# Attention with a two-layer network beside it on one core: filling matmuls at their whole length, unread products in half cycles that have none, rows of maxima sent one half cycle sooner, batches dealt by unit

## The chip, the cores and the metric

The kernel runs on one core of one Trainium2 chip. The metric is device time in microseconds (us) of one execution, lower is better. Before the change three runs took 1750.22, 1755.51 and 1757.24 us; their median is 1755.51 us. The engines are named as in the profile: PE is TensorE with its matmuls (PEld its weight loads), DVE is VectorE, ACT is ScalarE, POOL is GpSimd, and SP is SyncE, whose queue starts nearly all transfers.

## What is computed

One block of a transformer over 2048 rows of 512 numbers, in float32: a layer norm modulated by a condition, attention with 32 heads of 16 columns that share one key head and one value head, a gated residual, a second modulated layer norm, a gelu network of width 1376, and a second gated residual.

```python
mod = (_silu(c) @ w_mod).reshape(c.shape[0], 6, 1, -1)
sa, ca, ga, sb, cb, gb = (mod[:, 0], ..., mod[:, 5])
h = _layernorm(x, axis=-1) * (1 + ca) + sa
x = x + ga * _A_ref(h, A_wq, A_wk, A_wv, A_wo)     # softmax(q k^T / 4) v @ wo, 32 heads, one k and one v
h = _layernorm(x, axis=-1) * (1 + cb) + sb
x = x + gb * _B_ref(h, B_w1, B_b1, B_w2, B_b2)     # gelu(h @ w1 + b1) @ w2 + b2
```

## The kernel before the change

**Units and cycles.** After a prologue (keys, values, the first queries) the kernel runs 64 units: 8 blocks of 256 rows, and in each block 8 groups of four heads. A unit takes the 16 tiles of 128 keys in three cycles, by `GROUPS`: (3, 3), (2, 3) and (3, 2) tiles. A cycle has two half cycles. In each, PE makes score products `e` (L644, one for each key tile and each pair of heads s = 0 or 1), which ACT turns into exponentials `p` (L647), and products `m` (L542) for the maxima of a unit further on, which DVE reduces to one column (L547). An `e` or `m` product uses only 64 of the 128 rows of the array: s = 0 the upper half, s = 1 the lower. After each half cycle `pv` (L662) adds exponentials times values into the accumulator `acc`: 16 or 24 instructions in the trace. An x16 or x24 burst of `acc` on PE therefore marks the end of each half cycle.

**Filling.** While one half of the array makes the s = 1 products, the other half can do something else, and the next half cycle the other way round. What is put there is called the filling: the late query projections, and for a finished block the output projection `wo`, the second norm's transposes, and the two layers `w1` and `w2` (tiles `fill`, line L193). `compose(room)` (L1239) takes up to `room` products (256 columns each) from a queue of jobs; the room is given by `UNITS` for the three cycles of a unit. `halves` (L1491) issues the batch once on rows 0 to 63 and once on rows 64 to 127. The first filling of a half cycle waits for the exponential of the product `follow` (L1482) that closed the filling of the half before ("witness"), and for readers of the bank. Where a sum ends in a batch, `finish` (L1274) lets its reader run (ACT or DVE), after the second half's fillings; if the other sum of the bank is still under way, ACT also writes zeros there (L1285). Reductions of the last two maxima of such a half cycle are held until then.

**Order on PE.** `issue` (L1432) merges two lists by their nominal lengths: each `e` or `m` counts 1, a filling counts `AHEAD` times 0.5. With `AHEAD` = 0.75 the list of fillings runs through faster than the other one. `k` products `e` stand on the side of the filling, the rest beside it (`beside`, L1478); `k` is chosen so that the two sides have like lengths. The exponential of the last product beside the filling goes on ACT's queue only after the one of `follow`.

**A cycle with no filling** (`plain`, L1503) deals `m` and `e` of both halves in turn, and lends the filling's bank to one `m`.

**Maxima.** The maxima of a unit run ahead of its scores by 24 of 32 products (`LEAD`). When those of unit u are half done, `load_q(u + 1)` (L503) issues the eight transfers of the queries of the next unit on SP (L513 and L515, tile `qst`). When they are done, `put_max` (L566) reduces and transposes on DVE, gathers on POOL (L590, then the splits at L131 and L138) `MAX_WAIT[0]` ticks later (a tick is explained below), and sends four small transfers on SP (L585, `mh` and `ml`) `MAX_WAIT[1]` ticks after the transposition. The scores of unit u subtract these rows, so its first `e` waits for the last of them.

**Finished blocks.** When a block's last unit is done, `rest` fetches sums and outputs (`rsum` and `os`), inverts (`drs`), fetches the factors (`os<-drs`, L797), multiplies and splits on POOL (`norm`), and then feeds the filling. SP works strictly in the order of its queue: a transfer that waits for an engine, or for another transfer, holds all behind it. `later(n, fn)` calls fn after n ticks of a clock with four ticks for each cycle (two for each half cycle, one before and one after the `acc` burst).

Of the kernel before, what the change touches and what calls it, by code (L numbers as in the profile page):

```python
# [14 lines left out]
P = 128  # L15
# [14 lines left out]
MAX_WAIT = (1, 4)  # L30
QBUFS = 4
PREP = 4
BUSY = 3
BATCH = 6
GROUPS = ((3, 3), (2, 3), (3, 2))
UNITS = (16, 16, 14)
SPILL = 2
TAIL = (4, 8)
GROUP = 4
NORM_WAIT = 6  # L40
WARM = (4, 16, 2, 5)
MOD_WAIT = 3
AHEAD = 0.75
STIR = ((0, 4, 8, 12), (16, 32, 48, 0))


# [5 lines left out]
def adaln_mqa_mlp(  # L52
# [57 lines left out]
    ks = const.tile([P, S], F32R, name="ks")  # L110
# [35 lines left out]
    def later(n, fn):  # L146
        if draining[0]:
            fn()
        else:
            pending.append((clock[0] + n, fn))  # L150
# [38 lines left out]
    def half(one, s, behind=()):  # L189
# [4 lines left out]
        for other in behind:  # L194
# [3 lines left out]
    fill = {"bank": None, "next": 0, "flight": [None, None], "unread": [False, False], "bits": [True, True], "zero": [False, False],  # L198
            "reads": [], "last": None}
# [300 lines left out]
    NU = len(units)  # L500
# [123 lines left out]
    waiting = []  # L624
# [129 lines left out]
    def rest(b, fast):  # L754

        rp = wts_pool["rest"]
        row0, w = blocks[b]
        spread = ["m", "e", "m", "e", "m", "e", "v"] if fast else ["x"]
        turn = [0]

        def bank():
            turn[0] += 1
            tag = spread[turn[0] % len(spread)]
            return ebank() if tag == "e" else dict(tag=tag, bufs=3 if tag == "m" else 1)

        oss, ons = {}, {}

        def fetch():

            n = H * w // P  # L770
            rsum = att.tile([P, n], F32, name=f"rsum{b}", tag="rsum", bufs=1)
            nc.sync.dma_start(out=rsum, in_=do[b][:, :, 16, :].rearrange("q c (t n) -> (q c) t n", n=n))
            fetch_heads(0)

            def invert():
                nc.vector.reciprocal(out=rsum, in_=rsum)
                later(1, scatter)

            def scatter():
                nc.sync.dma_start(out=drs[b].rearrange("h (t n) -> (h t) n", n=n), in_=rsum)  # L780
                fetch_factors(0)

            later(4, invert)

        def fetch_heads(hf):

            os_ = oss[hf] = att.tile([P, 2, KD, HQ], F32, name=f"os{b}_{hf}", tag="opk", bufs=1)
            cols = slice(hf * HQ, (hf + 1) * HQ)
            for g in range(KD):
                src = do[b][2 * g:2 * g + 2, :, 0:16, cols].rearrange("q c r n -> (q c) r n")  # L790
                nc.sync.dma_start(out=os_[:, 0, g, :], in_=src)

        def fetch_factors(hf):
            cols = slice(hf * HQ, (hf + 1) * HQ)
            for g in range(KD):
                src = drs[b][8 * g:8 * g + 8, cols].unsqueeze(1).to_broadcast([8, 16, HQ])
                nc.sync.dma_start(out=oss[hf][:, 1, g, :], in_=src)  # L797
            later(7, lambda: norm(hf))

        def norm(hf):  # L800
            if fast:
                g = KD - 1
                split(state["on"][0][:, g, :], state["on"][1][:, g, :], state["os"][:, 0, g, :], nc.scalar, nc.vector)
                return
            onH = att.tile([P, KD, HQ], F32R, name=f"onH{b}_{hf}", tag="xH", bufs=2)
            onL = att.tile([P, KD, HQ], F32R, name=f"onL{b}_{hf}", tag="xL", bufs=2)
            ons[hf] = (onH, onL)
            os_ = oss.pop(hf)
            for g in range(KD):
                nc.gpsimd.tensor_tensor(out=os_[:, 0, g, :], in0=os_[:, 0, g, :], in1=os_[:, 1, g, :], op=ALU.mult)  # L810
            split(onH, onL, os_[:, 0], nc.gpsimd, nc.gpsimd)
            if (hf + 1) * HQ < w:
                later(6, lambda: (fetch_heads(hf + 1), fetch_factors(hf + 1)))
            ready[hf] = clock[0] + NORM_WAIT

        ready = {}
        later(*((4, lambda: norm(0)) if fast else (2, fetch)))
        return rest_steps(b, fast, rp, bank, ons, ready)

# [384 lines left out]
    pulled = []  # L1204
# [34 lines left out]
    def compose(cap):  # L1239

        batch, ends, used = [], [], 0
        while True:
            if not pulled:
                op = pull()
                if op is None:
                    break
                pulled.append(op)
            one, n = pulled[0]
            left = sum(units_of(b_) for _, _, b_ in one.ops[n:])
            if n == 0:  # L1250
                where = (0, 1) if one.wide else (fill["next"],)
                if any(fill["unread"][r] for r in where) or used and used + SPILL >= cap:
                    break
                begin = not any(fill["flight"])
                if begin:
                    fill["bits"][:] = [False, False]
                assert not one.wide or begin
                for r in where:
                    assert not fill["bits"][r] or fill["zero"][r]
                    fill["flight"][r], fill["unread"][r], fill["bits"][r], fill["zero"][r] = one, True, True, False  # L1260
                one.where = where[0]
                fill["next"] = 0 if one.wide else 1 - where[0]
            if used + units_of(one.ops[n][2]) > cap + (SPILL if used + left <= cap + SPILL else 0):
                break
            sub_, a, b_ = one.ops[n]
            ps = one.place()
            batch.append((ps if sub_ is None else ps[:, sub_], a, b_, n == 0 and begin, n == len(one.ops) - 1))
            used += units_of(b_)
            if n == len(one.ops) - 1:
                ends.append(one)  # L1270
            pulled.clear()
        return batch, ends, used / 2

    def finish(ends, ins):  # L1274
# [14 lines left out]
    first = [sum(size[:u]) for u in range(NU + 1)]  # L1289
    mp = Max()  # L1290
# [170 lines left out]
    behind = None  # L1461
    for u in range(NU):
        kt = 0
        for (nx, ny), room in zip(GROUPS, UNITS):
            X, Y = list(range(kt, kt + nx)), list(range(kt + nx, kt + nx + ny))
            kt += nx + ny
            goal = lead[u] + (lead[u + 1] - lead[u]) * kt / NKT
# [7 lines left out]
            def exps(s, which):  # L1475
                return [(1.0, lambda kt_=kt_: sexp(u, kt_, s)) for kt_ in which]

            def beside(s, which):  # L1478

                return exps(s, which[:-1]) + [(1.0, lambda: sexp(u, which[-1], s, None if followed else waiting))]  # L1480

            def follow(s, kt_):  # L1482

# [5 lines left out]
            ended, followed = [], []  # L1489
# [22 lines left out]
            batch, ends, long = compose(room) if behind else ([], [], 0)  # L1512
            if batch:
                k = min(max(1, round((n / 2 + nx + ny - long) / 2)), nx + ny - 1)
                which = X + Y
# [99 lines left out]
```

## Time and profile before

| | |
|---|---|
| runs | 1750.22, 1755.51, 1757.24 us (median 1755.51) |
| the profiled execution | 1755.45 us, its span 1753.6 us |
| mean granted PE clock | 0.969 |
| busy | PE 94%, PEld 64%, DVE 79%, ACT 73%, POOL 39% |
| cycles of the loop | 192, of which 16 without filling (15 after the first) |

The span is the time from the first to the last instruction. A "window" is a stretch of the span with the busy time of each engine in it and the granted clock; windows were laid on the ends of `acc` bursts, so that their lengths are the lengths of cycles or half cycles.

### The profile page before, as it was taken

To read this page: it belongs to the slowest core of one execution; us is meant where nothing else is said; L and a number is where in the kernel's file an instruction comes from. 1 tells how busy PE (TensorE), PEld (TensorE's weight loads), DVE (VectorE), ACT (ScalarE), POOL (GpSimd) and SP (SyncE) were. 2 spreads that over 40 slices of the span, in tenths; PEclk is the share of its full clock that TensorE was granted. 3 is DMA by queue.
4 is the path that set the end of the run, shared out by engine and by line. 5 is a ranking of instruction groups with operands and counts; after the bars stand their busy time and mean duration, and the time that the engine had idled before them with its cause. 6 is when DMAs were issued, how large, how long until landed. Compare 5 with 4: busy or idle time off the path is not lost.

```text
span 1753.6 us, 44436 instructions
## 1 busy us (share of the span) xinstructions
PE 1641.2 (94%) x17936; PEld 1125.2 (64%) x17936; DVE 1380.2 (79%) x2419; ACT 1271.5 (73%) x2564; POOL 682.5 (39%) x1194
## 2 busy tenths in 40 slices
PE   7999997999989998989989999889989999888998
PEld 4477763567765676657766677657766677555767
DVE  7888887888878887988878888788878788776524
ACT  6488876778766886778766887678867787666843
POOL 6335344556213462046322462135512362123630
PEclk9999999999998999999998999999999999988999
DMA  8125322212120211213012111203012121211241
GB/s 266 43 97 176 120 87 72 84 48 79 32 74 24 75 56 41 71 28 102 14 44 71 60 63 47 73 13 98 30 49 69 41 84 31 64 36 57 74 145 43
DMA packets 83138, 121.81 MB, mean 69 GB/s; under 512 B 19615, under 2 KB 56223, under 8 KB 82677
## 3 DMA queue, kind: packets, MB, share of 16 engines
q1 hardware_dynamic: 82916, 118.97, 20.8%
q8 instruction: 141, 2.31, 0.5%
q14 instruction: 65, 0.52, 0.1%
q10 hardware_dynamic: 16, 0.00, 0.0%
HBM read 91.13 MB, written 27.27 MB: 68 GB/s over the span
## 4 chain that ended last, share of the span: by engine, by line
PE 84%; ACT 5%; DVE 5%; SPq 2%; DMA 2%; issue 1%; POOL 1%; DVEq 0%; POOLq 0%
PE acc L662 27%; PE m L542 20%; PE fill L193 18%; PE e L644 15%; DVE mx L547 4%; ACT p L647 3%; SPq L585 1%; DMA qst<-ml 1%; PE w2ps L182 1%; PE w1ps L182 1%; DMA xt<-in_A_x_dram 1%; SPq L513 1%; PE fill L182 1%; PE kps L163 1%; ACT tt L1005 0%
## 5 line engine op out<-in xcount | busy, mean ns | idle before, releaser
L547 DVE TENSOR_REDUCE mx<-m 128x1 f32<-128x512 f32 x2016 | 1259.0, 684 | 278.9 <-PE m L542 156.9
L647 ACT ACTIVATE p<-e 128x512 f32<-128x512 f32 x2048 | 1087.6, 600 | 358.6 <-PE e L644 323.8
L644 PE MATMUL e<-qst,ks 64*128 64x512 f32 x2048 | 782.1, 442 | 67.1 <-DMA qst<-ml 41.2
L542 PE MATMUL m<-ks,qst 64*128 64x512 f32 x2016 | 809.6, 431 | 26.3 <-DVE mx L547 25.8
L662 PE MATMUL acc<-p,va 128*32 128x256 f32 x8192 | 534.6, 391 | 0.0
L542 PEld LDWEIGHTS m<-ks,qst 64*128 64x128 f32 x2016 | 369.6, 189 | 207.2 <-DVE mx L547 149.1
L644 PEld LDWEIGHTS e<-qst,ks 64*128 64x128 f32 x2048 | 340.6, 189 | 146.0 <-ACT p L647 86.6
L662 PEld LDWEIGHTS acc<-p,va 128*32 128x32 f32 x8192 | 230.0, 111 | 231.1 <-issue 110.9
L590 POOL TENSOR_SCALAR mt<-turned 8x32 f32<-8x32 f32 x256 | 53.1, 208 | 584.6 <-DVE turned L596 572.6
L193 PE MATMUL fill<-h2H,w1t 64*128 64x256 f32 x1232 | 233.6, 284 | 0.0
L193 PEld LDWEIGHTS fill<-h2H,w1t 64*128 64x128 f32 x1232 | 190.0, 186 | 0.1
L193 PE MATMUL fill<-h2L,w1t 64*128 64x256 f32 x616 | 173.1, 281 | 0.0
L193 PE MATMUL fill<-w2H,gH 64*128 64x256 f32 x560 | 164.0, 293 | 0.0
L193 PE MATMUL fill<-w2H,gL 64*128 64x256 f32 x560 | 162.4, 290 | 0.0
L193 PE MATMUL fill<-w2L,gH 64*128 64x256 f32 x558 | 158.4, 284 | 0.0
L193 PEld LDWEIGHTS fill<-h2L,w1t 64*128 64x128 f32 x616 | 114.7, 186 | 0.2 <-ACT p L647 0.2
L193 PEld LDWEIGHTS fill<-w2H,gL 64*128 64x128 f32 x560 | 107.4, 192 | 0.4
L193 PEld LDWEIGHTS fill<-w2H,gH 64*128 64x128 f32 x560 | 107.5, 192 | 0.0
L193 PEld LDWEIGHTS fill<-w2L,gH 64*128 64x128 f32 x558 | 106.8, 191 | 0.0
L1011 POOL TENSOR_TENSOR tt<-tt,z 128x256 f32<-128x256 f32 x77 | 56.5, 734 | 73.1 <-ACT tt L1005 73.1
L193 PE MATMUL fill<-woL,onH 64*128 64x256 f32 x224 | 63.7, 284 | 0.0
L193 PE MATMUL fill<-woH,onL 64*128 64x256 f32 x224 | 63.5, 283 | 0.0
(201 smaller groups left out, 1780.9 us busy)
## 6 DMA issues: line engine op xcount, KB each, us to landing
w1t<-dw SPq DMA_DIRECT2D x82, 512.0 KB
qst<-dq SPq DMA_DIRECT2D x384, 32.0 KB
do<-oc SPq DMA_DIRECT2D x64, 128.0 KB
dw<-w1s SPq DMA_DIRECT2D x11, 512.0 KB
xt<-in_A_x_dram SPq DMA_DIRECT2D x4, 1024.0 KB
dq<-qH SPq DMA_DIRECT2D x16, 256.0 KB
dq<-qL SPq DMA_DIRECT2D x16, 256.0 KB
x<-in_A_x_dram SPq DMA_DIRECT2D x8, 512.0 KB
```

The lines of the kernel that those rows point to most:

```text
L163: nc.tensor.matmul(ps, a, b_, start=begin and n == 0, stop=end and n == last)
L182: ins = nc.tensor.matmul(ps, a, b_, start=first_, stop=last_, **how)
L193: ins = nc.tensor.matmul(ps, a[rows], b_[rows], start=first_ and s == 0, stop=last_ and s == 1, skip_group_check=True)
L513: nc.sync.dma_start(out=raw(qst[64 * s + r:64 * s + r + 16]), in_=dq[h][g][part, a0 + s][:, :, cols])
L542: nc.tensor.matmul(m, qsts[u][rows, j, t * P:(t + 1) * P], ks[rows, kc * 512:(kc + 1) * 512], start=True, stop=True)
L547: nc.vector.tensor_reduce(out=self.mx[u][:, i, kc:kc + 1], in_=m, axis=AX.X, op=ALU.max)
L585: ring.dma_start(out=raw(dst), in_=raw(src[2 * T * s:2 * T * (s + 1), :].unsqueeze(1)))
L590: nc.gpsimd.tensor_scalar(out=mt[:, g:g + 32], in0=turned[g:g + 4 * T, :], scalar1=1.0, scalar2=0.0, op0=ALU.mult, op1=ALU.add)
L644: nc.tensor.matmul(e, ks[rows, kt * P:(kt + 1) * P], qst[rows].rearrange("p j n -> p (j n)"), start=True, stop=True)
L647: ins = nc.scalar.activation(slot(i), e, AF.Exp, scale=0.25)
L662: ins = nc.tensor.matmul(accs[u][32 * cidx:32 * cidx + 32, :], va[:, kt, :], slot(slots[u, kt, s])[:, j * w:(j + 1) * w], start=kt == 0, s ...
L1011: nc.gpsimd.tensor_tensor(out=tt, in0=tt, in1=z, op=ALU.mult)
```

## The change

- `AHEAD` goes from 0.75 to 1.0: a filling counts with its whole length when the order on PE is merged.
- In `compose`, a batch that would be empty, with no sum under way and maxima still to come, gets ten products of the keys with themselves that nobody reads (`IDLE`). They go through `halves` like any filling. With this 191 of the 192 cycles have a batch; seven of those hold only such products (in units 9, 11, 18, 27, 35, 51 and 59).
- `MAX_WAIT[1]` goes from 4 to 2: the four transfers `mh`, `ml` are put on SP's queue two ticks, one half cycle, sooner.
- The waits of a finished block shrink: `invert` from 4 to 3, `norm` from 7 to 5, `NORM_WAIT` from 6 to 5.
- `UNITS` depends on the unit: 12, 12, 12 products up to unit 8; 16, 16, 16 from 9; 16, 14, 14 from 22; 16, 16, 16 from 45.
- In `beside`, the last exponential is no longer put behind `follow`'s where k is over 1.

```diff
-MAX_WAIT = (1, 4)
+MAX_WAIT = (1, 2)
...
-UNITS = (16, 16, 14)
+UNITS = ((0, (12, 12, 12)), (9, (16, 16, 16)), (22, (16, 14, 14)), (45, (16, 16, 16)))
 SPILL = 2
+IDLE = 10
...
-NORM_WAIT = 6
+NORM_WAIT = 5
...
-AHEAD = 0.75
+AHEAD = 1.0
...
-            later(4, invert)
+            later(3, invert)
...
-            later(7, lambda: norm(hf))
+            later(5, lambda: norm(hf))
...
                 op = pull()
                 if op is None:
+                    if not batch and not any(fill["flight"]) and mp.done < first[NU]:
+                        idle = Sum([(None, ks[:, 0:P], ks[:, 0:256])] * IDLE, lambda one: None)
+                        pulled.extend((idle, i) for i in range(IDLE))
+                        continue
                     break
...
-            pulled.clear()
+            pulled.pop(0)
...
-        for (nx, ny), room in zip(GROUPS, UNITS):
+        for (nx, ny), room in zip(GROUPS, [rooms for since, rooms in UNITS if since <= u][-1]):
...
-                return exps(s, which[:-1]) + [(1.0, lambda: sexp(u, which[-1], s, None if followed else waiting))]
+                return exps(s, which[:-1]) + [(1.0, lambda: sexp(u, which[-1], s, None if followed or k > 1 else waiting))]
```

On SP's queue the change moves the rows of maxima past other transfers where a block has just been finished. What stands between the rows of unit 16 and those of unit 18 in program order:

```text
before: rows(16) | do rsum os(x4) out drs os<-drs(x4) loads(19) | rows(17) | do loads(20) | rows(18)
after:  rows(16) | loads(18) do rsum os(x4) out | rows(17) | drs os<-drs(x4) loads(19) do | rows(18)
```

## The prediction

> **What bounds the kernel now.** First the page: the span, busy time, and the chain that ended last by line.
>
> ```profile
> span 1753.6 us, 44436 instructions
> ...
> PE 1641.2 (94%) x17936; PEld 1125.2 (64%) x17936; DVE 1380.2 (79%) x2419; ACT 1271.5 (73%) x2564; POOL 682.5 (39%) x1194
> ...
> PE acc L662 27%; PE m L542 20%; PE fill L193 18%; PE e L644 15%; DVE mx L547 4%; ACT p L647 3%; SPq L585 1%; DMA qst<-ml 1%; PE w2ps L182 1%; PE w1ps L182 1%; DMA xt<-in_A_x_dram 1%; SPq L513 1%; PE fill L182 1%; PE kps L163 1%; ACT tt L1005 0%
> ```
>
> PE's products of the unit loop are the chain; the other engines appear with a few per cent each. As busy time says little about PE, I then laid windows on cycles (their ends are the ends of `acc` bursts): (2, 3) and (3, 2) of unit 29 and (3, 3) of unit 30, all with 16 fillings; (3, 2) of unit 31 with 14; (2, 3) of unit 43 with only four transposes; (3, 3) of unit 18 with 16, and of unit 7 with 18.
>
> ```profile
> 804.71:812.27 7.56, 7.56 (x94) 5.49 (x93) 6.47 (x12) 6.16 (x15) 4.15 (x10) 1.00 0.23 79
> 812.27:820.26 7.99, 7.99 (x102) 5.75 (x102) 6.17 (x10) 6.96 (x16) 4.86 (x8) 1.00 0.29 84
> 820.26:829.04 8.78, 8.65 (x98) 6.20 (x98) 7.55 (x12) 8.29 (x20) 5.83 (x10) 1.00 0.41 150
> 860.77:868.27 7.50, 7.50 (x99) 5.39 (x98) 6.63 (x11) 5.45 (x11) 0.00 (x0) 1.00 0.01 3
> 1158.66:1165.77 7.11, 6.58 (x78) 4.13 (x78) 6.20 (x12) 5.39 (x11) 2.02 (x7) 1.00 0.05 13
> 520.05:528.43 8.38, 8.38 (x99) 6.22 (x98) 7.89 (x14) 6.61 (x14) 0.00 (x0) 1.00 0.89 310
> 240.63:248.86 8.23, 8.23 (x101) 6.31 (x101) 7.41 (x14) 7.39 (x16) 4.84 (x6) 1.00 0.21 80
> ```
>
> Columns: length, then busy PE, PEld, DVE, ACT, POOL, clock, DMA. The third row is remarkable: in the w1 phase DVE (7.55) and ACT (8.29) fill most of 8.78 us, so a better order on PE can't gain without end there. The last two as well: 18 fillings take less time than 16.
>
> Next the same for what is not regular: the whole middle of the loop and its last units with maxima, then the first half cycles of units 17, 25, 33, 41, 49 and 57 (first of them, and the sum of the six).
>
> ```profile
> 319.60:1528.00 1208.40, 1146.31 (x13155) 792.79 (x13153) 997.00 (x1724) 911.50 (x1842) 457.54 (x842) 0.97 0.17 54
> 1528.00:1644.30 116.30, 102.67 (x1066) 67.30 (x1066) 85.03 (x151) 77.36 (x156) 40.55 (x74) 0.90 0.20 64
> ...
> 488.65:500.57 11.92, 6.71 (x48) 4.71 (x46) 4.00 (x6) 3.48 (x6) 3.91 (x3) 0.71 0.05 11
> ...
> sum 67.82, PE 37.49 PEld 26.90 DVE 23.08 ACT 20.57 POOL 24.27; mean PE 6.25 PEld 4.48 DVE 3.85 ACT 3.43 POOL 4.04
> ```
>
> A half cycle of this kind takes 4.03 us elsewhere (820.19 to 824.22 below), so the six cost 67.82 - 6 x 4.03 = 43.6 us. What is late there stands in the timeline of SP, POOL and the chain of waits:
>
> ```profile
> 478.99 0.44 POOL L138 TENSOR_TENSOR ml<-mt,mh 8x128 fp32r<-8x128 f32 x1
> ...
> 481.82 0.33 SPq L780 DMA_DIRECT2D drs<-rsum  x1
> 483.29 2.47 SPq L797 DMA_DIRECT2D os<-drs  x4
> 485.85 1.88 SPq L513 DMA_DIRECT2D qst<-dq  x3
> ...
> 490.70 0.43 SPq L515 DMA_DIRECT2D qst<-dz  x1
> 491.24 0.67 SPq L585 DMA_DIRECT2D qst<-mh  x1
> ...
> 493.32 1.61 DMA qst<-ml
> ```
>
> The rows of maxima were ready on POOL at 479.43, but went out from 491.24, behind the factors (`os<-drs`) and eight loads of queries; they landed at 494.93, 6.3 us after the half cycle could begin.
>
> **The change part by part.** *A, rows of maxima sooner.* In the new order rows(17) stand ahead of `drs`, so they can start at 479.5 and are out by 482.2 (491.24 to 493.89, 2.65 us). The old wait is gone: 43.6 us. But the loads of unit 19 are now late in their place: `drs` to `os<-drs` takes 1.47, the factors 2.56, the loads 5.39 (differences of the rows above), so they end at 482.2 + 9.4 = 491.6, and the last lands some 1.2 later, at 492.8. Their first reader is the fifth `m` of unit 17's first half cycle, about 2.0 us in (four `m` and four `e` of 512 columns ahead of it, each at twice the 0.12 us of a filling, 822.30 to 822.42 below), at 490.8. Where POOL is late with `ml`, SP now waits with these loads behind it, and the `m` of the next but one unit wait for them. PE's order holds all behind such an `m`, so some 2 us of wait remain, and some half clock behind it (0.71 in the row above): I take 3.5 us, for seven units (9, 17, ... 57), 24.5 us. Bounds: nothing left (gain 43.6), or each as dear as an old one (43.6 / 6), 7 x 7.3 = 51 (loss 7.5). A = -19. In units 60 and 61 sums and heads of the last block stand ahead of the rows in both orders, but no longer the loads: of the 116.30 us, 20.6 lie over four regular units (8.38 + 7.56 + 7.99 each), 12 of them beside the empty cycle counted in B; I take back 8 (0 to 12).
>
> *B, cycles without filling.* Fifteen of them, in eight windows (units 7 to 9 together, then seven single ones; first, two singles, last, and the sum), and the two half cycles of unit 19's:
>
> ```profile
> 248.86:319.61 70.75, 56.66 (x515) 26.59 (x514) 53.98 (x90) 44.67 (x86) 36.49 (x49) 0.95 0.28 87
> 343.60:353.10 9.50, 6.87 (x66) 3.27 (x66) 8.51 (x17) 6.68 (x13) 7.59 (x6) 1.00 0.09 27
> ...
> 1553.26:1570.20 16.94, 11.44 (x66) 4.81 (x66) 8.68 (x17) 6.91 (x13) 7.56 (x6) 0.64 0.04 12
> sum 153.10, PE 119.41 PEld 53.96 DVE 113.81 ACT 92.01 POOL 89.50; mean PE 14.93 PEld 6.74 DVE 14.23 ACT 11.50 POOL 11.19
> ...
> 543.94:549.12 5.18, 3.93 (x31) 1.64 (x30) 4.77 (x11) 3.15 (x6) 3.76 (x4) 0.86 0.00 0
> 549.12:556.26 7.14, 6.32 (x39) 2.62 (x38) 3.77 (x6) 3.65 (x7) 3.82 (x3) 0.50 0.18 49
> ```
>
> Nine are (3, 3), three (2, 3), three (3, 2). At the 8.38, 7.56 and 7.99 of filled ones they would take 122; so 31 us go. Some 11 of it is the halved clock: the (3, 3) of unit 11 takes 9.50 at full clock, that of unit 19 12.32, and there are four or five of the second kind. In their place stand cycles with a real batch or with ten unread products. These are 7 x 20 = 140 instructions more; beside `m` and `e` on the other half of the array they are hidden like any filling; uncovered, at 0.12 each (822.30 to 822.42 below), they cost 17. I count 2. B = -29 (-31 to -14).
>
> [...]
>
> *C, the order on PE.* What a half cycle looks like now (PE, unit 30; the last filling, then what is left, then `acc`, then the next half cycle; the last two rows are ACT's, at the end of that):
>
> ```profile
> 820.19 0.49 PE L542 MATMUL m<-ks,qst 64*128 64x512 f32 x1
> ...
> 822.30 0.28 PE L193 MATMUL fill<-h2H,w1t 64*128 64x256 f32 x1
> 822.42 0.46 PE L644 MATMUL e<-qst,ks 64*128 64x512 f32 x1
> 822.59 0.70 PE L542 MATMUL m<-ks,qst 64*128 64x512 f32 x2
> 823.22 1.07 PE L662 MATMUL acc<-p,va 128*32 128x256 f32 x16
> 824.22 0.49 PE L542 MATMUL m<-ks,qst 64*128 64x512 f32 x1
> ...
> 827.16 0.50 ACT L996 ACTIVATE z<-fill,b1c 128x256 f32<-128x256 f32 x1
> 827.70 0.38 ACT L1285 COPY fill<-mm 128x256 f32<-128x256 f32 x1
> ```
>
> Three fillings go for each product beside them, so the fillings end at 822.42 and two `m` run for 0.6 us with the other half of the array idle. With the whole length the order becomes two fillings for each product, and the last `m` stands beside the last filling. The best that this can give are the shortest cycles quoted: 7.11, 7.50 and 8.23, or 22.84 us for a unit. Units 10 to 57 take (1208.40 - 43.6 - 15.1) / 48 = 23.95, where 15.1 is what six empty cycles cost over filled ones (153.10 - 70.75 - 16.94 - 6 x 8.38); so at most 1.1 for each of 62 units, 69 us. Against it: the fillings end some 0.5 us later, and where a sum ends ACT's readers (0.50 + 0.38, 827.16 above) and the exponential that frees the next filling move with them. At up to 0.45 in each of the 154 cycles that end a sum that is a loss of 69. The row nearest to the new order is that with 18 fillings, whose fillings run longer beside the products and which ends two sums, and it gains 0.15 on the 8.38. I take -30, a little under half of the upper bound. The exponential that is no longer put back changes only ACT's order, at 73% busy: nothing; uncovered it is inside C's bounds.
>
> *D, batches and shorter waits of a block.* The same sums are made; in units 0 to 8 batches of twelve, one whole sum each, leave work for the cycles of units 7 to 9 that were empty (B). The shorter waits end in cycles that are filled in either case, and the earliest start of `wo` is hidden by the fillings behind it: nothing; if not hidden, one cycle of about 8 us a block is B's affair already.
>
> Sum, against the profiled execution (1755.45, 1.85 over its span, 0.06 under the median): 1755.45 - 19 - 8 - 29 - 30 = 1669, or **1670 us**.
>
> **The rivals.** *R1, the order gives nothing*, because DVE and ACT pace the half cycles (7.55 and 8.29 of 8.78): 1700. Against it, units with slack on both, as 860.77's. *R2, the late loads take the whole place of the late rows*: A = +7.5, 1696. For it: the factors and loads still follow each other as before. *R3, the clock falls anyway* in the cycles with dummies, and B loses 11: 1681. *R4, slower: the later end of the fillings.* Place: the first filling after a half cycle that ended a sum, which waits for the exponential behind `z` and the zeros. At the price of 0.45 in 154 cycles C is +69: 1769. It decides from 56 / 154 = 0.36 on, where all other gains (19 + 8 + 29) are eaten. For it: ACT's 8.29 of 8.78; against it, the 18-filling row.
>
> **How the numbers follow.** Forecast 0.58 (own range 1640 to 1700, C from -60 to 0); R1 0.16, R2 0.10, R3 0.06, R4 0.10. The range from 1635 to 1735 leaves out the upper half of R4 and C's whole bound. About 0.5% (9 us) is what a measurement of this kernel tells from no change. Faster by more 0.88 (all but R4 and a slip to its border), within 0.03, slower 0.09.
>
> **What would show it.** Right: the first half cycles of units 17 to 57 near 6 to 8 us, with PE waiting for `qst<-dq` rather than `qst<-ml`; no half clock in empty cycles; (2, 3) near 7.2 and (3, 2) near 7.6; the last `m` beside the last filling. Wrong: fillings that wait for ACT at the start of half cycles (R4), rows of maxima still behind loads, or regular cycles of unchanged length (R1).

## The result, and the profile after

| | before | after |
|---|---|---|
| runs | 1750.22, 1755.51, 1757.24 us | 1729.51, 1734.22, 1736.93 us |
| median | 1755.51 us | 1734.22 us, ratio 0.9882 (95% interval 0.9834 to 0.9929) |
| profiled execution | 1755.45 us, span 1753.6 us | 1736.93 us, span 1735.1 us |
| mean granted PE clock | 0.969 | 0.987 |

The change saves 21 us where 85 were forecast. Parts of it save more than the whole, and others give most of that back. All lines of the changed kernel behind the constants are one to some ten further down than before: `m` is L543 now, `e` L645, `acc` L663, the fillings L194.

From the page of the changed kernel, the span, the busy times and the chain by line:

```profile
span 1735.1 us, 44766 instructions
...
PE 1652.7 (95%) x18081; PEld 1122.3 (65%) x18081; DVE 1381.7 (80%) x2419; ACT 1261.2 (73%) x2556; POOL 682.4 (39%) x1194
...
PE acc L663 21%; PE m L543 16%; PE fill L194 12%; PE e L645 11%; ACT p L648 5%; DVE mx L548 5%; SPq L514 2%; DMA w1t<-dw 1%; POOL tt L1003 1%; DMA qst<-dz 1%; PE w1ps L183 1%; PE w2ps L183 1%; DMA xt<-in_A_x_dram 1%; SPq L798 1%; POOL z L1013 1%
```

PE is as busy as before, but its share of the chain is less: the loads of queries (L514, `qst<-dz`), of w1 (`w1t<-dw`) and POOL (L1003) have grown in it or come into it. Now windows on the same places as before: the six half cycles with the late rows of maxima (the first and the sum), then units 10 to 57 and 58 to 61.

```profile
494.88:501.17 6.29, 4.60 (x46) 2.93 (x46) 3.77 (x6) 3.15 (x6) 4.15 (x3) 0.89 0.12 26
...
sum 33.74, PE 25.42 PEld 17.29 DVE 22.70 ACT 18.92 POOL 23.36; mean PE 4.24 PEld 2.88 DVE 3.78 ACT 3.15 POOL 3.89
...
316.29:1518.13 1201.84, 1156.24 (x13254) 791.82 (x13254) 998.14 (x1723) 909.72 (x1846) 478.76 (x862) 0.99 0.18 58
1518.13:1627.93 109.80, 99.95 (x1095) 66.47 (x1094) 84.48 (x150) 77.14 (x158) 42.52 (x78) 0.95 0.20 62
```

The six half cycles went from 67.82 to 33.74 us, a gain of 34. Yet all of units 10 to 57 went only from 1208.40 to 1201.84: at least 27 us were lost again in the same units. SP's timeline shows what the first edit did (start, length, instruction):

```profile
485.11 0.67 SPq L586 DMA_DIRECT2D qst<-mh  x1
...
487.78 0.39 SPq L781 DMA_DIRECT2D drs<-rsum  x1
489.29 3.21 SPq L798 DMA_DIRECT2D os<-drs  x4
492.55 1.89 SPq L514 DMA_DIRECT2D qst<-dq  x3
...
496.97 0.43 SPq L516 DMA_DIRECT2D qst<-dz  x1
```

The rows of unit 17 now go out from 485.11, ten microseconds before the half cycle that needs them begins (494.88). The queries of unit 19, pushed behind the factors, are still being sent 2 us after that. What PE waits for, by waiting line and releaser (us in all, times, longest):

```profile
PE e L645 <- ACT p L648: 31.2, 92, 3.3
PE m L543 <- DMA qst<-dz: 14.7, 11, 3.1
PE m L543 <- DVE mx L548: 9.2, 25, 0.9
...
PE m L543 <- DMA qst<-dq: 7.9, 3, 3.5
```

The longest of PE's waits in the loop before was this one:

```profile
PE e L644 <- DMA qst<-ml: 41.2, 20, 4.7
```

`e` no longer waits for `ml`; `m` waits 22.6 us for queries instead. The longest single half cycle of the loop is new: the first one of unit 13, 12.2 us. Its piece of the chain:

```profile
389.40 1.25 POOL w2f L1196
...
391.43 1.30 POOL w2L L139
392.72 0.47 POOL w2f L1192
393.21 0.34 SPq L1193
...
397.87 1.58 DMA qst<-dz
```

A load of w2 (L1193) stands on SP's queue ahead of the queries and waits for the buffer that POOL is still splitting; the queries go out from 393.6, and the last piece lands at 399.45.

### The profile page after: what moved, and what is told of

The parts are those of the page before. It is cut to its first block, busy times and chain, and to the rows that moved or that the text cites. A ratio compares the mean times of both kernels' runs of the same rounds, so it can differ in the third digit from the quotient of the medians.

```text
span 1735.1 us, 44766 instructions
## 1 busy us (share of the span) xinstructions
PE 1652.7 (95%) x18081; PEld 1122.3 (65%) x18081; DVE 1381.7 (80%) x2419; ACT 1261.2 (73%) x2556; POOL 682.4 (39%) x1194
## 4 chain that ended last, share of the span: by engine, by line
PE 64%; ACT 8%; POOL 7%; issue 6%; DVE 6%; DMA 5%; SPq 5%; POOLq 0%; ACTq 0%; DVEq 0%
PE acc L663 21%; PE m L543 16%; PE fill L194 12%; PE e L645 11%; ACT p L648 5%; DVE mx L548 5%; SPq L514 2%; DMA w1t<-dw 1%; POOL tt L1003 1%; DMA qst<-dz 1%; PE w1ps L183 1%; PE w2ps L183 1%; DMA xt<-in_A_x_dram 1%; SPq L798 1%; POOL z L1013 1%
## 5 line engine op out<-in xcount | busy, mean ns | idle before, releaser
L548 DVE TENSOR_REDUCE mx<-m 128x1 f32<-128x512 f32 x2046 | 1274.4, 683 | 264.3 <-PE e L645 145.5
L543 PE MATMUL m<-ks,qst 64*128 64x512 f32 x2046 | 838.1, 431 | 34.6 <-DMA qst<-dz 14.7
L645 PE MATMUL e<-qst,ks 64*128 64x512 f32 x2048 | 798.8, 427 | 31.7 <-ACT p L648 31.2
L543 PEld LDWEIGHTS m<-ks,qst 64*128 64x128 f32 x2046 | 375.5, 186 | 257.7 <-DVE mx L548 157.6
L663 PE MATMUL acc<-p,va 128*32 128x256 f32 x8192 | 528.3, 387 | 0.0
L645 PEld LDWEIGHTS e<-qst,ks 64*128 64x128 f32 x2048 | 349.3, 187 | 101.1 <-ACT p L648 82.5
L663 PEld LDWEIGHTS acc<-p,va 128*32 128x32 f32 x8192 | 228.1, 110 | 208.3 <-issue 86.3
L194 PE MATMUL fill<-h2H,w1t 64*128 64x256 f32 x1232 | 248.6, 291 | 0.0
L194 PEld LDWEIGHTS fill<-h2H,w1t 64*128 64x128 f32 x1232 | 194.7, 186 | 2.8 <-ACT p L648 1.8
L194 PE MATMUL fill<-h2L,w1t 64*128 64x256 f32 x616 | 179.1, 291 | 0.0
L194 PE MATMUL fill<-w2H,gH 64*128 64x256 f32 x564 | 165.7, 294 | 0.0
L194 PE MATMUL fill<-w2H,gL 64*128 64x256 f32 x562 | 164.0, 292 | 0.1
L194 PE MATMUL fill<-w2L,gH 64*128 64x256 f32 x562 | 163.0, 290 | 0.0
L194 PEld LDWEIGHTS fill<-h2L,w1t 64*128 64x128 f32 x616 | 114.6, 186 | 0.7 <-ACT p L648 0.6
L194 PEld LDWEIGHTS fill<-w2H,gH 64*128 64x128 f32 x564 | 105.4, 187 | 0.4 <-ACT p L648 0.3
L194 PEld LDWEIGHTS fill<-w2H,gL 64*128 64x128 f32 x562 | 105.1, 187 | 0.7 <-POOL z L1013 0.4
L194 PEld LDWEIGHTS fill<-w2L,gH 64*128 64x128 f32 x562 | 104.8, 187 | 0.2
L194 PE MATMUL fill<-woH,onL 64*128 64x256 f32 x224 | 66.4, 296 | 0.0
L194 PE MATMUL fill<-woH,onH 64*128 64x256 f32 x224 | 65.7, 293 | 0.0
```

The lines of the kernel that those rows point to most:

```text
L194: ins = nc.tensor.matmul(ps, a[rows], b_[rows], start=first_ and s == 0, stop=last_ and s == 1, skip_group_check=True)
L543: nc.tensor.matmul(m, qsts[u][rows, j, t * P:(t + 1) * P], ks[rows, kc * 512:(kc + 1) * 512], start=True, stop=True)
L548: nc.vector.tensor_reduce(out=self.mx[u][:, i, kc:kc + 1], in_=m, axis=AX.X, op=ALU.max)
L645: nc.tensor.matmul(e, ks[rows, kt * P:(kt + 1) * P], qst[rows].rearrange("p j n -> p (j n)"), start=True, stop=True)
L663: ins = nc.tensor.matmul(accs[u][32 * cidx:32 * cidx + 32, :], va[:, kt, :], slot(slots[u, kt, s])[:, j * w:(j + 1) * w], start=kt == 0, s ...
```

## The experiments

Each ratio is to runs of the kernel before in the same job, whose medians were 1758.03, 1756.88 and 1756.11 us. "Class" below means cycles with the same tiles, number of fillings and `k`; their lengths are medians of one profiled execution over the units up to 61. One execution can lie well off the median: that of b_send took 1706.15 us at a mean clock of 0.991, that of send_mix 1730.99 at 0.980 and that of send_idle 1712.71 at 0.988, where the medians are 1713.52, 1719.72 and 1706.91.

### One part at a time

**b_send**: the kernel before with the rows of maxima two ticks sooner, nothing else.

```diff
-MAX_WAIT = (1, 4)
+MAX_WAIT = (1, 2)
```

> The kernel before, with MAX_WAIT = (1, 2) alone. Theory A: the six first half cycles of units 17 to 57 fall from 67.8 us together to 30 to 40, with waits for the loads of queries (qst<-dq) in place of qst<-ml; regular cycles unchanged; total -15 to -30 us. Rival: the loads take the whole place of the rows, six halves stay near 60 us, total unchanged within 5 us.

1713.52 us, ratio 0.9748 (0.9709 to 0.9787): **44 us saved**, twice what the whole change saves and more than the 15 to 30 expected. Its windows: the sum of the six half cycles, units 10 to 57, units 58 to 61, and the empty cycle (3, 3) of unit 19:

```profile
sum 34.02, PE 26.20 PEld 18.22 DVE 22.16 ACT 18.91 POOL 27.22; mean PE 4.37 PEld 3.04 DVE 3.69 ACT 3.15 POOL 4.54
...
319.87:1490.46 1170.59, 1129.37 (x13155) 784.75 (x13154) 995.41 (x1724) 909.79 (x1842) 459.00 (x842) 1.00 0.17 57
1490.46:1594.78 104.32, 97.25 (x1067) 64.94 (x1066) 84.73 (x151) 77.09 (x156) 40.69 (x74) 0.95 0.22 73
540.28:549.77 9.49, 7.01 (x66) 3.33 (x66) 8.53 (x17) 6.68 (x13) 7.59 (x6) 1.00 0.05 16
```

The half cycles give 33.8. A second gain was not in the sum at all: the empty cycle of unit 19, with the same 66 products, takes 9.49 us at full clock in place of 12.32 at 0.65 (0.50 in its second half cycle). The nine empty (3, 3) take 88.3 us together in place of 103.2. Regular cycles were not quite unchanged: the second half cycles of 36 (3, 3) with 16 fillings became 0.1 to 0.2 us longer, 5.8 us together.

**b_whole**: the kernel before with `AHEAD` 1.0, nothing else.

```diff
-AHEAD = 0.75
+AHEAD = 1.0
```

> The kernel before, with AHEAD = 1.0 alone. Theory Q (what stands on PE's queue behind a maximum product that waits for one of three banks waits with it, so the whole length helps only where k = 1): cycles (2, 3) with 16 fillings go from 7.55 to 7.28 us, (3, 2) with 16 from 7.98 to 7.7, but (3, 2) with 14 (k = 2) from 7.49 to 8.18 and (3, 3) with 16 from 8.37 to 8.47; the total within 0.5% of before. Rival X (the exponential that is no longer put back made the k = 2 cycles longer in the changed kernel): (3, 2) with 14 stays at 7.5 here, and the total falls by 15 to 25 us. Rival P (the prediction's C): all kinds get shorter, -30 us.

1780.92 us, ratio 1.0132 (1.0111 to 1.0153): **23 us lost**, where the forecast had 30 gained. Windows on the (2, 3) and (3, 2) of unit 29 (16 fillings, k = 1) and the (3, 2) of unit 31 (14 fillings, k = 2):

```profile
823.24:830.52 7.28, 7.28 (x93) 5.34 (x93) 6.35 (x12) 6.25 (x14) 3.96 (x10) 1.00 0.20 69
830.52:838.55 8.03, 8.03 (x103) 5.67 (x102) 6.37 (x11) 7.07 (x16) 5.07 (x9) 1.00 0.27 81
...
878.96:887.14 8.18, 8.18 (x98) 5.62 (x98) 6.62 (x11) 5.44 (x11) 0.00 (x0) 1.00 0.01 3
```

Before they took 7.56, 7.99 and 7.50. The 26 cycles (3, 2) with k = 2 cost 20.9 us together, nearly all of the loss, and more than theory Q had: thirteen of those with 14 fillings, which follow a (2, 3) with 16, take 8.7 us rather than 8.18 (send_mix shows why). Nor does k alone tell gain from loss. The (2, 3) with 18 fillings and k = 1 go from 7.42 to 7.76, the (3, 3) with 18 and k = 2 from 8.23 to 8.95, but the (3, 3) of unit 30, with 16 and k = 2, from 8.78 to 8.70.

**b_idle**: the kernel before with the unread products, nothing else (`IDLE = 10`, the four lines in `compose` and `pulled.pop(0)` of the change).

> The kernel before, with the ten unread products in half cycles without filling alone. Theory B: no half clock in these cycles any more, (3, 3) takes 10.4 us each where it took 9.5 at full clock or 12.3 with the fall, (2, 3) 7.8 or less for 8.16, (3, 2) 7.5 for 8.0; total -8 to -20 us. Rival (the clock falls anyway, by idle time): the 12.3 stay, total within 3 us or longer by some 5.

1746.43 us, ratio 0.993 (0.9912 to 0.9948): 12 us saved of the 29 forecast. Windows on the (3, 3) of unit 19 and the (2, 3) of unit 7, both with ten unread products:

```profile
545.59:555.54 9.95, 9.11 (x87) 5.29 (x86) 8.53 (x17) 6.62 (x13) 7.61 (x6) 1.00 0.10 28
...
250.55:257.72 7.17, 7.17 (x82) 4.69 (x82) 6.32 (x11) 5.33 (x10) 5.72 (x10) 1.00 0.19 74
```

The clock holds at 1.00 in seven of the nine (3, 3). In units 9 and 59, whose first half cycles wait for queries and for `ml` and take 8.4 and 9.1 us, it falls to 0.66 and 0.88. The (2, 3) and (3, 2) become shorter than empty (7.17 for 8.16, 7.60 for 8.00). But a (3, 3) takes 9.95: better than an empty one at half clock (12.32), worse than one at full clock (9.49), and far from the 8.38 of the forecast.

**a_ahead75**: the changed kernel with 0.75.

```diff
-AHEAD = 1.0
+AHEAD = 0.75
```

> The changed kernel with AHEAD back at 0.75. Theory Q: cycles (2, 3) with 16 fillings go back to 7.55 (from 7.28), those of 14 fillings, (2, 3) and (3, 2), fall from 7.75 and 8.18 to some 7.1 and 7.5, (3, 3) with 12 from 8.99 to 8.4 or less; total 10 to 25 us below the changed kernel. Rival X: 14 fillings stay at 7.75 and 8.18, total above the changed kernel by 10 to 20 us.

1713.94 us, ratio 0.9739 (0.9715 to 0.9763): the whole length costs 20 us by the medians in the changed kernel too. The loss is again mostly in cycles with k = 2: the (2, 3) and (3, 2) of this kind lose 22.8 us together. The 16 (2, 3) with 14 fillings lose most, from 7.06 to 7.75. The (3, 3) with 16 fillings gain 7.1 us. Here is the same half cycle of unit 23 in both kernels, a (2, 3) with the same 14 fillings (PE, then DVE). First the changed kernel:

```profile
657.91 0.49 PE L543 MATMUL m<-ks,qst 64*128 64x512 f32 x1
...
659.78 0.49 PE L543 MATMUL m<-ks,qst 64*128 64x512 f32 x1
659.78 0.38 PE L194 MATMUL fill<-w2L,gH 64*128 64x256 f32 x1
...
660.12 0.28 PE L194 MATMUL fill<-w2H,gL 64*128 64x256 f32 x1
660.24 0.39 PE L645 MATMUL e<-qst,ks 64*128 64x512 f32 x1
660.56 1.50 PE L663 MATMUL acc<-p,va 128*32 128x256 f32 x24
...
658.44 3.08 DVE L548 TENSOR_REDUCE mx<-m 128x1 f32<-128x512 f32 x5 [0.77 <-PE e L645]
```

Then with 0.75:

```profile
653.37 0.50 PE L543 MATMUL m<-ks,qst 64*128 64x512 f32 x1
...
655.24 0.28 PE L194 MATMUL fill<-w2H,gL 64*128 64x256 f32 x1
655.25 0.49 PE L543 MATMUL m<-ks,qst 64*128 64x512 f32 x1
655.37 0.38 PE L645 MATMUL e<-qst,ks 64*128 64x512 f32 x1
655.68 1.50 PE L663 MATMUL acc<-p,va 128*32 128x256 f32 x24
```

The fifth and last `m` starts 1.87 us after the first in one kernel (657.91 to 659.78) and 1.88 in the other: it has to wait until DVE has reduced the second (five reductions take 3.08 us, three banks hold the products), and neither of the two orders on PE changes that. What differs is what stands behind it. With 0.75 that is one `e`, and `acc` starts 0.43 later. With 1.0 it is three fillings and the `e`, though the fillings run on the other half of the array and use another bank; the last filling starts 2.21 us after the first `m` where with 0.75 it starts 1.87 after it, and `acc` starts 0.78 after the last `m`. That is 0.35 for a half cycle, 0.70 for a cycle, and the cycles differ by 0.69 (7.75 and 7.06 in windows on this one). With 16 fillings in a (2, 3) it is otherwise. There the last `m` starts 2.24 us after the first with 0.75 and 1.96 with 1.0, with no filling behind it (medians), so the order does move it, and the half cycle is 0.13 shorter.

### Only where it helps

**a_mix**: the changed kernel with the whole length only where k = 1.

```diff
-                return [(AHEAD * units_of(one[2]) / 2, lambda
+                return [((1.0 if k == 1 else 0.75) * units_of(one[2]) / 2, lambda
```

> The changed kernel with a filling counted at its whole length only in cycles with k = 1, and at 0.75 in all others. Theory Q (PE's queue keeps its order, and with the whole length the fillings and the last e stand behind an m that waits for a reduction of DVE; only where k is 1 nothing is queued behind it): in units 0 to 61 the cycles of k = 1 keep what they have in the changed kernel ((2, 3) 7.29, against 7.55 at 0.75), the others go back ((2, 3) with k = 2 from 7.75 to 7.05, (3, 2) with k = 2 from 8.18 to 7.5); summed over the cycles about 20 us under the changed kernel, 6 under the one with 0.75 everywhere: 1708 us against the 1714 and 1734 measured. Rival (the whole length gains nowhere by itself; the 0.27 us of k = 1 are given back in the next cycle): same as 0.75 everywhere, 1714. Rival (what the whole length costs is shared by all cycles, as DVE or ACT get late): half of it stays, 1724.

1713.97 us, ratio 0.9755 (0.9726 to 0.9784). The classes are as theory Q had them: (2, 3) with k = 1 takes 7.28, with k = 2 7.05, and (3, 2) with k = 2 7.5. The 6 us that this should have brought over 0.75 everywhere do not show in the time, which is that of the first rival; they are no more than its uncertainty.

**send_mix**: the same edit in the kernel of b_send.

> The kernel before with two edits: the rows of maxima two ticks sooner, and a filling counted at its whole length in cycles with k = 1 alone. Theory Q: the 52 cycles (2, 3) with k = 1 take 7.28 for 7.55 and the twenty (3, 2) with k = 1 stay at 7.98 to 8.03, as with the whole length everywhere; the rest is as in the kernel with only the rows sooner (1713.5 in its runs): 1707. Rival (the gain is given back): 1713. If the whole length in the cycles of k = 1 alone were what cost the 23 us: 1730 or more.

1719.72 us, ratio 0.98 (0.9768 to 0.9832), not the 1707 expected; that it is longer than b_send is not shown either, as the intervals overlap. In the two profiled executions the 52 cycles (2, 3) gain 7.9 us, as expected, but the 26 (3, 2) that follow such a cycle lose 7.8 though their own order is unchanged. All of that lies in the first half cycles of the thirteen that come behind 16 fillings and have 14 (4.4 us for 3.75 to 3.9). There the gain is given back. Here is what PE waits for in that of unit 2, which begins at 140.42, and what stands ahead on ACT:

```profile
141.27 0.50 PE L644 MATMUL e<-qst,ks 64*128 64x512 f32 x1 [0.42 <-ACT p L647]
...
139.42 0.37 ACT L488 COPY q<-fill 128x256 f32<-128x256 f32 x1 [0.16 <-PE e L644]
139.82 0.38 ACT L1285 COPY fill<-mm 128x256 f32<-128x256 f32 x1
140.13 2.75 ACT L647 ACTIVATE p<-e 128x512 f32<-128x512 f32 x5
```

The next product, and the first filling with it, waits for an exponential that stands behind ACT's reader of an ended sum and the zeros, which is the place that R4 named. PE's waits of this kind (L644 for L647) are 31.3 us in all, against 25.8 in b_send. In the same way the first half cycles of some thirteen (3, 3) with 16 fillings lose 0.3 each. The nine empty cycles take 96.8 us in place of 88.3, at a lower clock (0.84 for 1.00 in that of unit 19); as these two executions lie on opposite sides of their medians, it says nothing of the edit (the other runs of both have mean clocks from 0.982 to 0.990).

**send_idle**: b_send and b_idle together.

> The kernel before with two edits: the rows of maxima two ticks sooner, and the unread products in cycles without filling. Theory (the fall of the clock in empty cycles was mostly a consequence of the stalls behind late rows, so that the two gains are partly the same): only the shorter (2, 3) and (3, 2) are left to gain, 3 times 1.0 and 3 times 0.4, and (3, 3) loses 0.2 to 0.4 each: 1709 to 1714, against 1713.5 for the rows sooner alone. Rival (the gains add up): the 11.7 us that the products gave by themselves come in full, 1702.

**1706.91 us**, ratio 0.9718 (0.9687 to 0.9748), the best of all runs by its median, and between the two expectations. By the medians the unread products bring 7 us on top of the sooner rows (5 by the ratios), in place of the 12 that they bring alone; the intervals overlap. In the profiled executions they gain 3.3 us in three (2, 3) and 1.2 in three (3, 2), and lose 7.4 in nine (3, 3), 4.1 of it in unit 9, where the first half cycle takes 7.8 us. These sum to a loss, so the traces do not bear out the gain by the medians.

### Batches and waits

**a75_u**: the changed kernel with 0.75 and the old rooms.

```diff
-UNITS = ((0, (12, 12, 12)), (9, (16, 16, 16)), (22, (16, 14, 14)), (45, (16, 16, 16)))
+UNITS = ((0, (16, 16, 14)),)
```

> The changed kernel with 0.75 and with the old room of every unit (16, 16, 14), so that against the kernel before it has the rows sooner, the unread products, the shorter waits of a block and the exponential that is no longer put back; against the changed kernel with 0.75 (1713.9) only the dealing is undone. Theory (the dealing costs: more cycles hold a real batch, the w2 loads are prepared where the queries of unit 13 are loaded, 12.2 us in one half cycle): that half cycle goes back to about 4, and the time to 1704 to 1709. Rival (the dealing is free, as in the prediction's part D): 1714. Rival (it gains, and the shorter waits of a block cost): over 1718.

1724.38 us, ratio 0.981 (0.9778 to 0.9842). A miss: the last rival was right. The dealing gains, 10 us against a_ahead75; unit 13 does go back to 4.0 us without it, but other units are longer (10 and 50, for instance, 7.3 and 8.9). And the short waits of a block must cost some 17 against send_idle. SP's timeline in unit 18:

```profile
504.29 0.44 SPq L831 DMA_DIRECT2D x<-in_A_x_dram  x1
504.78 2.77 SPq L825 DMA_DIRECT2D w1t<-dw  x3
507.59 1.93 SPq L514 DMA_DIRECT2D qst<-dq  x3
```

**a75_u_w**: the same with the old waits of a block.

```diff
-            later(3, invert)
+            later(4, invert)
...
-            later(5, lambda: norm(hf))
+            later(7, lambda: norm(hf))
...
-NORM_WAIT = 5
+NORM_WAIT = 6
```

> The changed kernel with 0.75, the old room of every unit and the old waits of a block (4, 7, 6): against the kernel before it has the rows sooner, the unread products and the exponential that is no longer put back. Theory W (the shorter waits bring x and three w1 loads ahead of the next queries on SP's queue, in units 10, 18, 26, 34, 50 and 58, where the first half cycle took 5.2 to 10.0 us): these six go back to 4.0, and the time to that of the two edits alone, 1704 to 1710, 17 under the 1724 with the short waits; PE waits some 13 us for queries in place of 27. Rival (the exponential is what cost the 17): 1724 stays, with the long half cycles gone or not.

1708.13 us, ratio 0.9721 (0.9694 to 0.9747): as send_idle, 16 under a75_u. The same place on SP's queue:

```profile
507.77 1.87 SPq L514 DMA_DIRECT2D qst<-dq  x3
...
514.32 0.43 SPq L831 DMA_DIRECT2D x<-in_A_x_dram  x1
514.79 1.44 SPq L825 DMA_DIRECT2D w1t<-dw  x3
```

With the short waits a block's `x` and its first three w1 tiles stand directly ahead of the next queries, with the old ones 6.5 us behind their first. The windows on the first half cycles of units 10, 18, 26, 34, 50 and 58 sum to 42.75 us with the short waits and 24.79 with the old ones. Since the exponential that is no longer put back is in both kernels and not in send_idle, it costs nothing that can be measured, as forecast.

**a75_u_f2**: the short waits stay, but `x` and w1 are put on the queue two ticks later.

```diff
-        nc.sync.dma_start(out=x1, in_=xf[row0:row0 + w, :].rearrange("(t p) d -> p t d", p=P))
         w1ts = {}
-        for f in range(3):
-            fetch_w1(b, w1ts, f)
+        def fetch_all():
+            nc.sync.dma_start(out=x1, in_=xf[row0:row0 + w, :].rearrange("(t p) d -> p t d", p=P))
+            for f in range(3):
+                fetch_w1(b, w1ts, f)
+        if b < len(blocks) - 1:
+            later(2, fetch_all)
+        else:
+            fetch_all()
```

> The same with the short waits kept, but x and the first three w1 loads of a block put on SP's queue two ticks later, behind the next queries. Theory W: place on the queue is all that the short waits cost; the six first half cycles go back to 4.0 to 4.5 and the time to 1705 to 1712. Rival (the loads compete for the DMA engines wherever they stand, or POOL and DVE are late by the earlier work): half or more of the 17 us stays, 1716 to 1724.

1709.16 us, ratio 0.973 (0.9704 to 0.9755): 14 of the 16 us are back. Place on SP's queue is what the short waits cost. Unit 10 did not go back (9.1 us): there DVE sits idle for 4.62 us before it adds `x` (L921, at 313.68), whose load goes out only at 309.96. The next run shows the same wait.

**a_mix_f2**: the same two ticks in a_mix.

> The changed kernel with the whole length only where k = 1, and with x and w1 two ticks later. Theory W: the first half cycles of units 18, 26, 42 and 58 (6.7, 7.6, 5.8, 8.5) go back to 4.0, about 12 us under the 1714 of the same kernel without the later loads: 1702. Unit 13 keeps its 12 us. Rival as above: 1708 to 1714.

1715.46 us, ratio 0.9757 (0.973 to 0.9783): a miss, nothing gained. Units 42 and 58 went back as expected, but 18 and 26 became longer, 10.8 and 10.0 us (6.7 and 7.6 in a_mix). There the sum of `wo` ends before `x` has come, and its reader needs `x`. DVE's timeline in unit 18:

```profile
509.52 1.89 DVE L548 TENSOR_REDUCE mx<-m 128x1 f32<-128x512 f32 x3 [0.77 <-PE m L543]
516.23 0.42 DVE L921 TENSOR_TENSOR x<-fill,x 128x256 f32<-128x256 f32 x1 [4.83 <-DMA x<-in_A_x_dram]
516.57 1.28 DVE L548 TENSOR_REDUCE mx<-m 128x1 f32<-128x512 f32 x2
```

The addition of `x` waits 4.83 us for the late load, and two reductions, whose banks PE needs, stand behind it. The wait that was taken from the queries has gone to DVE.

**a_mix_f2_d**: the same with the old rooms up to unit 8.

```diff
-UNITS = ((0, (12, 12, 12)), (9, (16, 16, 16)), (22, (16, 14, 14)), (45, (16, 16, 16)))
+UNITS = ((0, (16, 16, 14)), (9, (16, 16, 16)), (22, (16, 14, 14)), (45, (16, 16, 16)))
```

> The kernel of the run before this one with the old room (16, 16, 14) up to unit 8 and the new dealing from unit 9. Theory (batches of twelve up to unit 8 leave queries to project until unit 9, put the preparation of w2 off to units 10 to 13, and its loads, which wait for POOL, hold the queries that unit 13 needs: 12 us in one half cycle): this half cycle goes back to 4.0 and gains 8; six more cycles of units 7 to 10 get unread products in place of a batch and lose 0.1 to 1.5 each, 3 together: 1697. Rival (the wait goes to another unit, as w2 has to be prepared at some time): 1702 or more.

1724.68 us, ratio 0.9818 (0.9792 to 0.9844): a miss, 9 lost where 5 were expected to be gained. Unit 13 did go back, but the first half cycles of units 10 and 12 now take 10.8 and 8.7 us. In unit 12 it is as the rival had it: a load of w2 waits for POOL until 371.86, ahead of the queries. In unit 10 it is not w2 but the late `x` again: DVE sits idle for 4.96 us before it adds `x` (at 319.86), whose load went out from 315.64. So this run does not show that the preparation of w2 makes someone wait wherever it falls.

## Why the prediction was wrong

The ladder of kernels, each a step from the one above it; the differences are between ratios, times 1755.5 us, each uncertain by 7 to 10 us:

| step | ratio | step's part | forecast |
|---|---|---|---|
| rows of maxima sooner (b_send) | 0.9748 | -44 | A and units 60, 61: -27 |
| unread products (send_idle) | 0.9718 | -5 | B: -29 |
| the exponential (a75_u_w) | 0.9721 | 0 | 0 |
| shorter waits of a block (a75_u) | 0.981 | +16 | D: 0 |
| dealing (a_ahead75) | 0.9739 | -12 | D: 0 |
| whole length (after) | 0.9882 | +25 | C: -30 |

The parts sum to -20, and 21 were measured. That 1734 lies just inside the range of 1635 to 1735 is luck: C missed by 55 us, and D, taken as nothing, was +16 and -12. Each part is worth this only at its place in the ladder. The dealing, above all, gains beside the short waits as they are; with the loads put back on the queue, a_mix_f2 (new dealing and the order of a_mix, 1715.46 us) takes no less time than a75_u_f2 (old rooms, 1709.16).

- **C failed, and its sign with it.** The failing step is "the last `m` stands beside the last filling" as a gain. In the cycles that lose, the start of the last `m` is set by DVE's reductions, 1.87 us after the first, in either order. Putting fillings behind it in PE's queue makes them wait too: three of them, 0.35 us, where there are 14. The step holds where the last `m` started later than that: in a (2, 3) with 16 fillings it gained 0.27 (7.28 for 7.55), in a (3, 2) with 16 nothing, and in a (3, 3) with 16 up to 0.2 in the changed kernel (8.47 for 8.67 in unit 30). The row with 18 fillings, taken as nearest to the new order, was no evidence: with the whole length the same class is longer (8.95 for 8.23 in b_whole). R1 named the right engine, DVE, but as a pace for the cycle, which would have cost nothing. R4 had the sign, with 69 us for C where 25 were measured, and the place of a part: PE's waits for exponentials (L644 for L647) grew from 24.4 us to 33.8 in b_whole. The larger part, fillings behind an `m` that waits for its bank, it did not have.
- **A was right in its mechanism and mis-sized.** The old wait went, and a new one for queries came, on the tiles named. The term "3.5 us, for seven units" was too large: the six half cycles keep (34.02 - 6 x 4.03) / 6 = 1.6 us each in b_send. In the profiled run of b_send the empty cycles also keep the full clock for the most part (1.00 in those of units 19, 35 and 51, for 0.65, 0.64 and 0.66 before), 15 us that the forecast had put under B. That the sooner rows are the cause is likely but not shown: in the kernel before, the empty cycles of units 27 and 43 kept the full clock too (9.50 us each), behind half cycles of 10.8 and 10.6 us with late rows. What the sum left out is the 5.8 us that the (3, 3) with 16 fillings lost. R2 falls: the late loads did not take the whole place of the late rows. In units 58 to 61 the gain is 12.0 us (116.30 to 104.32 in b_send) where 8 were taken; the empty cycle of unit 59 is half of it.
- **B failed in the term "at the 8.38, 7.56 and 7.99 of filled ones".** A (3, 3) with few fillings is not as long as one with 16. The trace of before had the nearer row: six of its seven (3, 3) with six fillings take 9.71 to 9.74. A window of the kernel before on that of unit 20:

```profile
571.58:581.30 9.72, 8.55 (x78) 4.54 (x78) 7.57 (x13) 6.68 (x13) 2.58 (x5) 1.00 0.04 13
```

  With 9.72 in place of 8.38 for nine cycles B would have been 12 us smaller, -17. In b_idle the wait in unit 9 takes another 5.7 (15.21 for 9.49), which leaves -11, near the -12 measured. Beside A less is left, as most of the halved clock is gone already in the profiled run of b_send; the -5 of the ladder is too uncertain to settle it. That the unread products hold the clock was right in seven of nine cycles (1.00), so R3 falls but for units 9 and 59 (0.66 and 0.88, with first half cycles of 8.4 and 9.1 us).
- **D was no zero.** "The shorter waits end in cycles that are filled in either case" left out SP's queue: an earlier norm means earlier loads of `x` and w1, ahead of the queries. It is the same kind of conflict as in A, and it was missed because only the waits themselves were costed, not the transfers that they release. The dealing gains beside these loads, with a long wait of its own (unit 13, 12.2 us).
- **Of the signs to look for**, the half cycles near 6 to 8 us with a wait for queries came (4.5 to 7.7). (2, 3) near 7.2 came with 16 fillings (7.28) but not with 14 (7.75). (3, 2) near 7.6 came neither with 16 nor with 14 (8.08 and 8.19); the 7.28 and 7.71 of those with 12 fillings are no sign, as with 0.75 they take 7.03 and 7.47.

What stays open: which of the three shorter waits of a block would do alone; why the gain that is given back in send_mix is mostly kept in a_mix; whether the unread products gain anything beside the sooner rows; and what decides whether an empty cycle falls to half clock.

## What to carry to other kernels

Before a matmul is moved ahead of others in one queue, find what its start hangs on. In the half cycles with 14 fillings it was a bank that DVE frees: nothing was won by issuing the `m` sooner (it started 1.87 us after the first in one order, 1.88 in the other), and what was put behind it was late with it, 0.35 us for a half cycle. Keep independent work ahead of such an instruction, not behind. Cost an earlier step by the transfers that it releases and by their place on the queue; four small transfers behind others cost 44 us here, slower clock included, and `x` and three w1 tiles ahead of the queries 16. And estimate a part-filled stage from a row that is part-filled.

## What the runs showed of the hardware

In the half cycles looked at, PE started matmuls in the order issued, also across the two halves of its array: in that of unit 23 with 1.0 the last three fillings, on the free half, started with or behind an `m` that waited for its bank, and the last of them 0.34 us later than with 0.75 (2.21 and 1.87 us after the first `m`). With it `acc` starts 0.35 us later in this half cycle with 14 fillings (0.78 us after the last `m` for 0.43). In the stretches of SP's queue shown here, transfers went out in the order issued: in unit 13 of the changed kernel a load of w2 (L1193) went out only at 393.21, when POOL was done, and the queries behind it from 393.60.

The granted clock of one and the same cycle was not a property of the cycle. With 66 products and 2.5 us of idle time in 9.49 us (9.49 - 7.01), unit 19's empty cycle ran at full clock in b_send and at 0.65 before, with the stall of unit 17 (11.92 us in one half cycle) some 43 us earlier. Such a stall did not decide it. In the kernel before, unit 27's empty cycle ran at full clock (9.50 us, 1.00) at the same distance behind a half cycle of 10.80 us in unit 25. In b_whole unit 35's ran at 1.00 behind one of 11.25 in unit 33, and unit 19's at 0.65 behind one of 10.46. In the profiled run of send_mix unit 19's ran at 0.84 behind one of only 6.26. What did decide it no run shows.
